# Two of three score banks to ScalarE, the third to VectorE, with new loads and planner constants, in a four-block attention kernel

## The chip, the cores and the metric

The kernel runs on one core of a Trainium2 chip. The metric is the device time of one execution in microseconds (us); lower is better. A core has engines that run side by side, each through its own list of instructions, in order: TensorE (PE, matrix products; PEld is its weight load), VectorE (DVE), ScalarE (ACT, functions such as exp), GpSimd (POOL), and the queues that start DMA transfers (SP, and ACT's own). An instruction waits on semaphores for what it needs, and everything behind it on its engine waits with it.

## The reference

x is 2048 x 1024 in bf16. Four blocks follow each other: A, B, A, B with the same weights for both A and for both B. Each has a layer normalisation before it and adds its result to x.

```
def A(x, wqkv, w_phi, wo):                  # linear attention, 32 heads of 32
    q, k, v = heads(x @ wqkv)
    pq, pk = q @ w_phi[h], k @ w_phi[h]
    phi_q = concat(softmax(pq), softmax(-pq));  phi_k likewise
    kv = phi_k^T v;  z = sum_s phi_k
    return ((phi_q kv) / (phi_q z + 1e-6)) @ wo
def B(x, wqkv, wo):                         # softmax attention, 32 heads of 32
    q, k, v = heads(x @ wqkv)
    return (softmax(q k^T / sqrt(32)) v) @ wo
```

## The kernel before

**One planner writes the order.** Nothing in the program is placed by hand. Each step is recorded as an `Op` with an engine, an assumed duration, dependencies, buffers and a priority. `Sched.run` then plays through time: an engine that is free takes the ready op of the lowest priority value whose buffers can be had, and the order in which it takes them is the order in which the instructions are emitted. On-chip memory is one arena from which buffers are cut, with a quota for each class; the accumulators are eight PSUM banks of 128 x 512 f32. The constants at the top (`LAT`, `act_us`, `dve_us`, `MM`, `MM4`) are what the planner assumes of latencies and durations. Where PE would be idle too long, the planner emits a filler: four column matmuls against a constant (`idle_acc` at L1377, or `idle` with onesD).

**Stages.** Work goes by chunks of 512 positions (four) and by groups of four heads (eight). In a linear block (A), `layernorm`, `a_keys`, `a_queries` and `a_out` run full 128 x 128 matmuls (helper line L481); q and k weights have w_phi folded in at the start (`fold_phi`: PE transposes L613, copies L617, products L636, evacuations L643 and L646). x comes in transposed by `load_x` (L516), chunk 0 first, chunks 1 to 3 in one piece for each of eight row blocks. The weights that PE transposes come on ACT's queue in two halves of rows (L604). Quota "mm" is the number of banks that the products of `a_queries` and `a_out` may hold.

**Attention (B).** Scores are computed transposed: keys on partitions, queries along the free dimension. A unit is one head, 128 keys, 512 queries: one matmul of 32 rows, one bank. A turn is a query chunk with a group of four heads, 64 units (two pairs of heads `pp`, eight key blocks `d`, four units `j`); there are 32 turns in each attention. Units are gathered by threes: three matmuls on three row strips (L1101) into banks 0 to 2 or 3 to 5 in turn, and one exponential of 1536 elements on ScalarE (L1110), into a buffer E. Products with v and the sums of the denominator are column matmuls, four at a time (L1142), accumulating in bank 6, which VectorE copies out at the end of each half turn (L1158). Bank 7 serves the projections that run beside attention (helper line L485).

**VectorE's share.** `EXTRA` names for each turn the pairs (pp, d) whose units j = 2 and 3 are not ScalarE's. `exp_dve` computes their exponentials on VectorE: for each of the two units a single score matmul into bank 7 (L1037), issued "along" a score group on another row strip, and a read that adds a bias and clamps (L1044); then for both together two integer steps (L1047, L1050), three polynomial steps (L1055) and a last product (L1058). The fields `along` and `rows` and the constants `AGAIN` and `DUE` make the planner place the single matmul beside a score group.

Of the kernel before, what the change touches and what calls it, by code (L numbers as in the profile page):

```python
# [10 lines left out]
ACT = mybir.ActivationFunctionType  # L11
# [23 lines left out]
class Op:  # L35
    __slots__ = ("eng", "dur", "lat", "fn", "bufs", "prio", "mode", "ndep", "out", "t", "start", "seq", "accum", "first", "ahead", "along", "drain", "rows")

    def __init__(self, eng, dur, lat, fn, bufs, prio, mode, seq):
        self.eng, self.dur, self.lat, self.fn, self.bufs = eng, dur, lat, fn, bufs
        self.prio, self.mode, self.seq = prio, mode, seq  # L40
        self.ndep, self.out, self.t, self.start, self.accum, self.first, self.ahead, self.along, self.drain = 0, [], 0.0, None, None, False, 0.0, False, False
        self.rows = ()


LAT = {"PE": 0.25, "ACT": 0.2, "DVE": 0.1, "POOL": 0.2, "SP": 2.0, "AQ": 2.0}
SWITCH = 0.1
AGAIN = 0.2
# [4 lines left out]
class Sched:  # L52
# [99 lines left out]
    def run(self):  # L152
# [21 lines left out]
        rows = ()  # L174
        started = {}
        for o in self.ops:
            if o.ndep == 0:
                heapq.heappush(ready[o.eng], (not (o.first or o.along), o.prio - o.ahead, o.seq, o))
        now = -100.0
        t, left, order = 0.0, len(self.ops), []  # L180
        while left:
            moved = False
            for e in engines:
# [5 lines left out]
                while ready[e] and len(skipped) < 400:  # L189
# [11 lines left out]
                    if item[3].along and (mode[e] != item[3].mode or item[3].rows[0] in rows) and item[3].prio > now - DUE:  # L201
                        skipped.append(item)
                        continue
# [25 lines left out]
                if pick.first:  # L229
                    now = pick.prio  # L230
# [5 lines left out]
                if pick.along and (mode[e] != pick.mode or pick.rows[0] in rows):  # L236
                    d += AGAIN
                if e == "PE":
                    rows = pick.rows
# [15 lines left out]
                heapq.heappush(events, (t + d, n, pick, True))  # L255
# [12 lines left out]
            while events and events[0][0] <= t + 1e-9:  # L268
                _, _, o, own = heapq.heappop(events)
                if not own:  # L270
                    for b in o.bufs:
                        b.left -= 1
                        if b.left == 0:
                            self._release(b)
                for x in o.out:
# [4 lines left out]
                    if x.ndep == 0:  # L280
                        heapq.heappush(ready[x.eng], (not (x.first or x.along), x.prio - x.ahead, x.seq, x))
# [15 lines left out]
DUE = 0.0  # L297
# [4 lines left out]
QUOTA = {"pk": 3, "pv": 2, "kv": 1, "ln": 2, "mm": 2, "cmp": 2, "bc": 4, "num": NUMS, "wt": 4, "fil": 2,  # L302
# [3 lines left out]
         "xs": 1, "xu": 2, "xg": 1, "xx": 1, "E1": 3}  # L306
# [14 lines left out]
EXTRA = (lambda i: [(0, 2), (1, 2)] if 10 <= i < 19 else [(1, 2)] if 2 < i < 31 else [],  # L321
         lambda i: [(0, 1), (0, 5), (1, 3)] if 10 <= i < 26 and i % 2 else [(0, 3), (1, 3)] if 1 <= i < 30 else [])


def act_us(n):
    return n / 1200 + 0.064


def dve_us(n):
    return n / 960 + 0.15  # L330


MM = 0.2165
# [3 lines left out]
def kernel(  # L337
# [150 lines left out]
    MM4 = 0.225  # L488
# [22 lines left out]
    def load_x():  # L511
        for lo, hi, prio, us in ((0, 1, -15.0, 1.3), (1, NC, -9.0, 2.0)):
            last = []
            for po in range(PO):
# [3 lines left out]
                    issue=us, kb=128))  # L518
# [8 lines left out]
    def layernorm(c, prio, banks, alone=False, n=2):  # L527
# [7 lines left out]
        for h in range(n):  # L535
# [6 lines left out]
            else:  # L542
                halves.append(op(
                    "DVE", 2048 / 1920 + 0.15, lambda hs=hs: nc.vector.tensor_tensor(
# [55 lines left out]
    def fold_phi(col, wd_v, prio, use_pe):  # L600
        w_t = []
        if use_pe:
            nb, nv = sb("wnat", PO, D)
            ld = [dma(-20.0, lambda h=h: nc.scalar.dma_start(  # L604
                out=nv()[:, 4 * h:4 * h + 4, :], in_=A_w[:, 4 * h:4 * h + 4, col:col + D]),
                (), [nb], q="AQ", kb=1024) for h in range(2)]
            for g in range(G):
                tb, tv = ps("wt", ANY)

                def tr(g=g, tv=tv):  # L610
# [4 lines left out]
                t1 = op("PE", 8 * 0.11, tr, ld, [tb, nb], prio, mode="n")  # L615
                wb, wv_ = sb("wT", D)
                t2 = op("ACT", act_us(1024), lambda tv=tv, wv_=wv_: nc.scalar.copy(  # L617
                    out=wv_(), in_=tv().bitcast(BF16)), [t1], [tb, wb], prio)
# [8 lines left out]
        for fc in range(2):  # L627
            s_b, s_v = sb("slab", PO, C512)
            parts = []
            for m in range(PO):  # L630
# [8 lines left out]
                a = op("PE", 4 * 0.1, fn, [w_t[4 * fc + k][2] for k in range(4)] + phi_ld,  # L639
# [384 lines left out]
    def exp_dve(qc, g, pp, d, prio, kT, q_of):  # L1024
# [7 lines left out]
        for k in range(2):  # L1032
            s_b, s_v = ps("xs", FIL)

            def sfn(k=k, s_v=s_v):
                r = slice(64 + 32 * k, 96 + 32 * k)
                nc.tensor.matmul(  # L1037
                    out=s_v(), lhsT=kT[g][1]()[r, pp, d * P:(d + 1) * P],
                    rhs=q_of[(qc, g)][1]()[r, (pp + 1) % 2, :], start=True, stop=True,
                    tile_position=(64 + 32 * k, 0))  # L1040
            so = op("PE", 0.05, sfn, flat([kT[g][2][d // 2], q_of[(qc, g)][2]]),
                    [s_b, kT[g][0], q_of[(qc, g)][0]], prio, mode="r")
            so.along, so.rows = True, (2 + k,)
            ys.append(op("DVE", dve_us(512), lambda k=k, s_v=s_v: nc.vector.tensor_scalar(  # L1044
                out=y_v()[:, k, :].bitcast(I32), in0=s_v(), scalar1=POW2_B, scalar2=0.0, op0=ALU.add, op1=ALU.max),
                [so], [s_b, y_b], prio + 0.01))
        mo = op("DVE", 1024 / 1920 + 0.15, lambda: nc.vector.tensor_scalar(  # L1047
            out=m_v().bitcast(I32), in0=y_v().bitcast(I32), scalar1=0x7FFFFF, scalar2=0x3F800000,
            op0=ALU.bitwise_and, op1=ALU.bitwise_or), ys, [y_b, m_b], prio + 0.02)
        po = op("DVE", 1024 / 1920 + 0.15, lambda: nc.vector.tensor_scalar(  # L1050
            out=y_v().bitcast(I32), in0=y_v().bitcast(I32), scalar1=0x7F800000, scalar2=None,
            op0=ALU.bitwise_and), [mo], [y_b], prio + 0.02)
        last = [mo]
        for i, c in enumerate(POW2_C):
            last = [op("DVE", dve_us(1024), lambda i=i, c=c: nc.vector.scalar_tensor_tensor(  # L1055
                out=x_v(), in0=(x_v() if i else m_v()), scalar=c, in1=m_v(), op0=ALU.add, op1=ALU.mult),
                last, [m_b, x_b], prio + 0.02)]
        eo = op("DVE", dve_us(1024), lambda: nc.vector.scalar_tensor_tensor(  # L1058
            out=e_v(), in0=x_v(), scalar=POW2_0, in1=y_v(), op0=ALU.add, op1=ALU.mult),
            [po, *last], [x_b, y_b, e_b], prio + 0.02)  # L1060
        return eo, (e_b, lambda: e_v().rearrange("p a b -> p (a b)"))

    def attention(base, kT, vT, q_of, gate, extra):
# [6 lines left out]
        ex_of, e_of = {}, {}  # L1070
        for qc, g in turns:
            for pp, d in extra(pos[(qc, g)]):
                eo, (e_b, e_v) = exp_dve(qc, g, pp, d, base + 10 * pos[(qc, g)] + 5 * pp + 0.5 * d - LEAD, kT, q_of)
                for k in range(2):
                    ex_of[(qc, g, pp, d, 2 + k)] = eo
                    e_of[(qc, g, pp, d, 2 + k)] = (e_b, e_v, k)
        units = [u for u in units if u not in ex_of]
        n = 0
        while units:
            grp = []  # L1080
            for u in units[:LOOK]:
                if len(grp) < WIDE and u[4] not in [v[4] for v in grp]:
                    grp.append(u)
            w = len(grp)
            units = [u for u in units if u not in grp]
# [327 lines left out]
```

## Time and profile before

| | us |
|---|---|
| median of three runs (2389.13 to 2389.97) | 2389.96 |
| profiled execution | 2389.32 |
| its span, first to last instruction | 2387.5 |
| PE busy | 2245.1 |
| ScalarE busy | 2077.7 |
| VectorE busy | 1646.7 |

Busy time is the union of an engine's instructions. Matmuls are pipelined and fillers count, so PE's figure is no measure of useful work; PE's busy time and matmul durations overlap from one to the next. Instructions of ScalarE overlap too: the duration of one is longer than the distance to the next. In a row of groups the columns are line, engine, operation, output and input, form, count, then busy us and mean ns of one, then the engine's idle time before them and what ended it. In a row of the timeline they are start, length, engine, line, operation, count, and idle time before.

### The profile page before, as it was taken

Reading aid. Unit: us, or ns where it says so; the run is one execution under the profiler, and the core shown is the slowest. Engines: PE = TensorE matmul, PEld = TensorE weight load, DVE = VectorE, ACT = ScalarE, POOL = GpSimd, SP = SyncE. Lnnn points to the kernel's source line nnn. Section 1 sums busy time; section 2 is a strip of 40 time slices with the busy share of each in tenths; the row PEclk is TensorE's granted clock in tenths of the full one; section 3 lists DMA queues with packets and bytes.
Section 4 is the critical chain, followed back from the end, with each engine's and each line's share of the span. In section 5 each row is a group of like instructions: output and inputs, shape, how many; then the busy total and the mean of one; then the engine's idle time right before and its main releaser. Section 6 shows DMA issues by size and latency. Waiting matters only on the chain.

```text
span 2387.5 us, 65441 instructions
## 1 busy us (share of the span) xinstructions
PE 2245.1 (94%) x28960; PEld 845.8 (35%) x28960; DVE 1646.7 (69%) x2107; ACT 2077.7 (87%) x1856; POOL 25.7 (1%) x70
## 2 busy tenths in 40 slices
PE   7999999999999999999998999999999999989998
PEld 4443343333333333333333434433333333333333
DVE  6987752345577767666665776477778888978763
ACT  6336549999999999999997555899999999999998
POOL 0000000000000000000000000000000000000000
PEclk9999999999999999999999999999999999999999
DMA  9120101112231121222413101011111100111111
GB/s 213 50 50 1 32 14 36 30 38 54 57 90 55 46 69 55 81 68 81 130 57 107 37 5 32 22 32 31 34 26 37 37 20 24 55 36 34 39 36 37
DMA packets 216805, 118.58 MB, mean 50 GB/s; under 512 B 138952, under 2 KB 206536, under 8 KB 215752
## 3 DMA queue, kind: packets, MB, share of 16 engines
q1 hardware_dynamic: 215464, 112.29, 17.6%
q8 instruction: 226, 3.70, 0.6%
q10 hardware_dynamic: 1056, 2.10, 0.3%
q14 instruction: 59, 0.48, 0.1%
HBM read 78.71 MB, written 14.14 MB: 39 GB/s over the span
## 4 chain that ended last, share of the span: by engine, by line
ACT 45%; PE 33%; issue 10%; DVE 7%; DMA 3%; SPq 2%; ACTq 0%; DVEq 0%
ACT arena L1110 42%; PE psum L481 17%; PE psum L485 5%; PE psum L1142 4%; PE psum L1101 4%; DMA arena<-rd 2%; DVE arena L1055 2%; ACT arena L685 1%; SPq L516 1%; DVE arena L1199 1%; DMA arena<-arena 1%; DVE arena L1044 1%; PE psum L854 1%; PE psum L718 1%; DVE arena L577 0%
## 5 line engine op out<-in xcount | busy, mean ns | idle before, releaser
L1110 ACT ACTIVATE arena<-psum 128x1536 bf16<-128x1536 f32 x1297 | 1751.5, 1687 | 21.1 <-PE psum L1101 17.0
L1142 PE MATMUL psum<-arena 128*32 128x512 bf16 x4096 | 627.4, 385 | 10.6 <-DVE arena L1158 9.3
L1142 PE MATMUL psum<-arena,ones_bf 128*32 128x512 bf16 x4096 | 627.6, 385 | 0.0
L1101 PE MATMUL psum<-arena 32*128 32x512 bf16 x3890 | 512.6, 383 | 84.6 <-ACT arena L1110 74.3
L485 PE MATMUL psum<-arena 128*32 128x512 bf16 (+1 forms) x8768 | 581.2, 376 | 9.3 <-DVE arena L917 3.6
L481 PE MATMUL psum<-arena 128*128 128x512 bf16 (+1 forms) x2032 | 454.9, 374 | 13.6 <-ACT arena L685 4.4
L1101 PEld LDWEIGHTS <-arena 32*128 32x128 bf16 x3890 | 173.8, 91 | 586.9 <-issue 576.1
L1055 DVE SCALAR_TENSOR_TENSOR arena<-arena 128x1024 f32<-128x1024 f32 x309 | 377.0, 1220 | 4.3
L481 PEld LDWEIGHTS <-arena 128*128 128x128 bf16 x2032 | 190.5, 98 | 255.3 <-issue 55.5
L485 PEld LDWEIGHTS <-arena 128*32 128x32 bf16 x8768 | 195.7, 96 | 237.5 <-issue 117.1
L1142 PEld LDWEIGHTS <-arena 128*32 128x32 bf16 x4096 | 167.0, 95 | 252.1 <-issue 196.5
L1044 DVE TENSOR_SCALAR arena<-psum 128x512 int32<-128x512 f32 x206 | 141.8, 688 | 94.0 <-PE psum L1037 81.5
L917 DVE CAST arena<-psum 128x512 bf16<-128x512 f32 x120 | 82.6, 689 | 168.8 <-PE psum L485 153.5
L1142 PEld LDWEIGHTS <-ones_bf 128*32 128x32 bf16 x4096 | 163.7, 95 | 30.9 <-issue 12.1
L1058 DVE SCALAR_TENSOR_TENSOR arena<-arena 128x1024 bf16<-128x1024 f32 x103 | 125.7, 1221 | 4.1 <-PE psum L1142 0.2
L1377 PE MATMUL psum<-xT,zero 128*32 128x512 bf16 x1412 | 114.4, 381 | 0.0
L685 ACT ACTIVATE arena<-psum 128x512 bf16<-128x512 f32 x80 | 42.9, 600 | 82.1 <-PE psum L481 65.6
L689 DVE TENSOR_REDUCE arena<-arena 128x32 f32<-128x1024 bf16 x64 | 77.8, 1215 | 44.5 <-ACT arena L685 44.1
L1199 DVE TENSOR_TENSOR arena<-arena 64x512 bf16<-64x512 f32 x124 | 84.7, 683 | 33.5 <-DMA arena<-rd 31.9
L1158 DVE COPY arena<-psum 128x512 f32<-128x512 f32 x126 | 86.3, 685 | 26.3 <-PE psum L1142 25.8
L811 ACT ACTIVATE arena<-psum 128x512 bf16<-128x512 f32 x128 | 69.5, 595 | 33.3 <-PE psum L481 32.7
L573 DVE TENSOR_TENSOR arena<-xT,arena 128x1024 f32<-128x1024 bf16 x64 | 77.9, 1220 | 24.2 <-ACT arena L562 24.0
(101 smaller groups left out, 1363.3 us busy)
## 6 DMA issues: line engine op xcount, KB each, us to landing
arena<-rd SPq DMA_DIRECT2D x62, 256.0 KB
arena<-in_B_wqkv_dram SPq DMA_DIRECT2D x48, 256.0 KB
arena<-in_A_wqkv_dram SPq DMA_DIRECT2D x10, 1024.0 KB
arena<-arena SPq DMA_DIRECT2D x256, 32.0 KB
arena<-in_B_wo_dram SPq DMA_DIRECT2D x32, 256.0 KB
arena<-wd_k SPq DMA_DIRECT2D x8, 1024.0 KB
arena<-arena SPq DMA_DIRECT2D x96, 64.0 KB
arena<-in_B_wqkv_dram SPq DMA_DIRECT2D x4, 1024.0 KB
```

What stands on the lines that cost most here:

```text
L481: nc.tensor.matmul(out_, lhsT=lhsT, rhs=rhs, start=start, stop=stop, skip_group_check=True)
L485: nc.tensor.matmul(out_[ks, :], lhsT=lhsT[:, ks], rhs=rhs, start=start, stop=stop, tile_position=(0, 32 * k), skip_group_check=True)
L917: return op("DVE", dve_us(512), lambda: nc.vector.tensor_copy(out=dst(), in_=src()), [dep], bufs, prio)
L1044: ys.append(op("DVE", dve_us(512), lambda k=k, s_v=s_v: nc.vector.tensor_scalar(out=y_v()[:, k, :].bitcast(I32), in0=s_v(), scalar1=POW2_B ...
L1055: last = [op("DVE", dve_us(1024), lambda i=i, c=c: nc.vector.scalar_tensor_tensor(out=x_v(), in0=(x_v() if i else m_v()), scalar=c, in1=m_ ...
L1058: eo = op("DVE", dve_us(1024), lambda: nc.vector.scalar_tensor_tensor(out=e_v(), in0=x_v(), scalar=POW2_0, in1=y_v(), op0=ALU.add, op1=ALU ...
L1101: nc.tensor.matmul(out=s_v()[:, x * C512:(x + 1) * C512], lhsT=kT[g][1]()[r, pp, d * P:(d + 1) * P], rhs=q_of[(qc, g)][1]()[r, (pp + j // ...
L1110: ex = op("ACT", act_us(w * C512), lambda s_v=s_v, e_v=e_v, w=w: nc.scalar.activation(out=e_v()[:, 0:w * C512], in_=s_v(), func=ACT.Exp, s ...
L1142: nc.tensor.matmul(out=a_v()[col:col + 32, :], lhsT=v_v()[:, kc % 4, o:o + DH] if what == 0 else ones_bf[:], rhs=ev()[:, x * C512:(x + 1) ...
L1158: cp = op("DVE", dve_us(512), lambda t_v=t_v, a_v=a_v: nc.vector.tensor_copy(out=t_v(), in_=a_v()), [last], [a_b, t_b], prio - 4)
L1199: s = [op("DVE", dve_us(512), lambda a=a, k=k, o_v=o_v, r_v=r_v, T=T: nc.vector.tensor_tensor(out=o_v()[a, :], in0=T[k][1]()[a, :], in1=r_ ...
L1377: nc.tensor.matmul(psum[32 * k:32 * k + 32, 6 * C512:7 * C512], lhsT=zero[:], rhs=xT[:, 0, 0:C512], start=False, stop=False, tile_position ...
```

## The change

- **Score groups.** A unit of VectorE's no longer has a bank and a matmul of its own. Any three units make a group, with at most one of VectorE's among them, and that one is put last, in the group's third bank. ScalarE's exponential then covers the first two banks (1024 elements) and VectorE's read takes the third, at the priority of the bank evacuations. `along`, `rows`, `AGAIN`, `DUE` and buffer class "xs" go.
- **VectorE's share.** `EXTRA` gives (0, 1) and (1, 1) to nearly every turn: 51 pairs in the first attention (37 before) and 60 in the second (66 before).
- **Durations.** The planner's constants are new, among them the fixed part of a VectorE instruction (0.067 us for 0.15) and of a ScalarE instruction (0.052 for 0.064), the latencies from ScalarE and VectorE to others (0.17 for 0.2, 0.18 for 0.1), and a latency of an engine to itself (`OWN`), which was none.
- **Loads.** x's chunk 0 gets a priority ahead of the phi loads, chunk 1 is loaded by itself, chunks 2 and 3 together. W's two halves are column halves, so that a transpose group waits for one half. VectorE takes every other evacuation of these transposes.
- **Banks.** The quota "mm" is 4 in place of 2.

```diff
-LAT = {"PE": 0.25, "ACT": 0.2, "DVE": 0.1, "POOL": 0.2, "SP": 2.0, "AQ": 2.0}
+LAT = {"PE": 0.25, "ACT": 0.17, "DVE": 0.18, "POOL": 0.2, "SP": 2.0, "AQ": 2.0}
+OWN = {"PE": 0.0, "ACT": 0.15, "DVE": 0.1, "POOL": 0.1, "SP": 0.0, "AQ": 0.0}
...
-                    if item[3].along and (mode[e] != item[3].mode or item[3].rows[0] in rows) and item[3].prio > now - DUE:
-                        skipped.append(item)
-                        continue
...
-                heapq.heappush(events, (t + d, n, pick, True))
+                heapq.heappush(events, (t + d, n, None, True))
+                n += 1
+                heapq.heappush(events, (t + d + OWN[e], n, pick, True))
...
-"mm": 2
+"mm": 4
...
-EXTRA = (lambda i: [(0, 2), (1, 2)] if 10 <= i < 19 else [(1, 2)] if 2 < i < 31 else [],
-         lambda i: [(0, 1), (0, 5), (1, 3)] if 10 <= i < 26 and i % 2 else [(0, 3), (1, 3)] if 1 <= i < 30 else [])
+EXTRA = (lambda i: [(0, 1), (1, 1)] if 8 <= i < 31 else [(1, 1)] if 2 < i < 31 else [],
+         lambda i: [(0, 1), (1, 1)] if 1 <= i < 31 else [])
 def act_us(n):
-    return n / 1200 + 0.064
+    return n / 1200 + 0.052
 def dve_us(n):
-    return n / 960 + 0.15
+    return n / 960 + 0.067
-MM = 0.2165
+MM = 0.2157
-    MM4 = 0.225
+    MM4 = 0.215
...
-        for lo, hi, prio, us in ((0, 1, -15.0, 1.3), (1, NC, -9.0, 2.0)):
+        for lo, hi, prio, us, kb in ((0, 1, -24.0, 1.3, 128), (1, 2, -9.0, 1.3, 400), (2, NC, -8.0, 2.0, 800)):
...
-                out=nv()[:, 4 * h:4 * h + 4, :], in_=A_w[:, 4 * h:4 * h + 4, col:col + D]),
+                out=nv()[:, :, C512 * h:C512 * h + C512], in_=A_w[:, :, col + C512 * h:col + C512 * h + C512]),
...
-                t1 = op("PE", 8 * 0.11, tr, ld, [tb, nb], prio, mode="n")
+                t1 = op("PE", 8 * 0.1, tr, [ld[g // 4]], [tb, nb], prio, mode="n")
...
+                if g % 2:
+                    t2 = op("DVE", dve_us(1024), lambda tv=tv, wv_=wv_: nc.vector.tensor_copy(
+                        out=wv_(), in_=tv().bitcast(BF16)), [t1], [tb, wb], prio)
...
+        def by_dve(u):
+            return u[:4] in ours and u[4] >= 2
...
-                if len(grp) < WIDE and u[4] not in [v[4] for v in grp]:
+                if len(grp) < WIDE and u[4] not in [v[4] for v in grp] and not (
+                        by_dve(u) and any(by_dve(v) for v in grp)):
                     grp.append(u)
+            units = [u for u in units if u not in grp]
+            grp.sort(key=by_dve)
             w = len(grp)
+            wa = sum(not by_dve(u) for u in grp)
...
-            so = op("PE", 0.24, sfn, deps + (gate if n == 0 else []), [s_b, *bufs], prio - 2, mode="r")
+            so = op("PE", 0.222, sfn, deps + (gate if n == 0 else []), [s_b, *bufs], prio - 2, mode="r")
...
-            ex = op("ACT", act_us(w * C512), lambda s_v=s_v, e_v=e_v, w=w: nc.scalar.activation(
-                out=e_v()[:, 0:w * C512], in_=s_v(), func=ACT.Exp, scale=math.log(2) / BITS),
+            ex = op("ACT", act_us(wa * C512), lambda s_v=s_v, e_v=e_v, w=wa: nc.scalar.activation(
+                out=e_v()[:, 0:w * C512], in_=s_v()[:, 0:w * C512], func=ACT.Exp, scale=math.log(2) / BITS),
...
+                if by_dve(u):
+                    read, rest, _, de_b, de_v = pair[u[:4]]
+                    read(u[4] - 2, so, s_b, lambda s_v=s_v, x=x: s_v()[:, x * C512:(x + 1) * C512], prio - 2)
```

In the changed file the score matmuls are L1094, the exponential L1102, the read of the third bank L1029, the two integer steps L1036 and L1039, the polynomial L1044 and L1047, the products with v L1143.

117 lines of the change are left out of this document (52 added, 65 removed).

## The prediction

> **What bounds the kernel now.** I read the page first, then busy time by stage, then the groups by line, then single stretches of the timeline.
>
> ```profile
> span 2387.5 us, 65441 instructions
> ACT  6336549999999999999997555899999999999998
> ACT 45%; PE 33%; issue 10%; DVE 7%; DMA 3%; SPq 2%; ACTq 0%; DVEq 0%
> ...
> 0.00:356.00 356.00, 334.33 (x2951) 151.14 (x2952) 264.49 (x364) 180.38 (x291) 11.04 (x38) 0.99 0.26 60
> 356.00:1287.40 931.40, 875.53 (x12748) 308.65 (x12747) 562.93 (x710) 916.19 (x718) 12.10 (x24) 0.99 0.24 66
> 1287.40:1506.00 218.60, 210.44 (x1581) 89.26 (x1580) 154.86 (x213) 117.53 (x201) 2.58 (x8) 1.00 0.08 25
> 1506.00:2376.00 870.00, 818.02 (x11628) 294.13 (x11626) 657.75 (x812) 862.33 (x646) 0.00 (x0) 1.00 0.13 33
> ...
> L1110 ACT ACTIVATE arena<-psum 128x1536 bf16<-128x1536 f32 x1297 | 1751.5, 1687 | 21.1 <-PE psum L1101 17.0 <-PE psum L1142 3.4 <-PE psum L1037 0.3
> L1377 PE MATMUL psum<-xT,zero 128*32 128x512 bf16 x1412 | 114.4, 381 | 0.0
> ```
>
> The stage rows give the stretch, then busy time of PE, weight load, VectorE, ScalarE, GpSimd. There are four stages: the linear layer (0 to 356), attention, the second linear layer (1287 to 1506), attention. In both attentions ScalarE is busy 916 of 931 us and 862 of 870; the chain names ScalarE's exponential (L1110) first, and its idle time in the whole run is 21.1 us. PE is busy nearly as long by the row, but 1412 of its matmuls (L1377) are filler against zeros. So attention lasts as long as ScalarE's work plus its stalls, and a linear stage as long as PE's work plus PE's waits.
>
> **Sum, term 1: ScalarE's exponentials.** Duration (1687 ns) is not pitch, because one starts before the last has ended. Runs of one form give the pitch.
>
> ```profile
> 1688.65 19.00 ACT L1110 ACTIVATE arena<-psum 128x1536 bf16<-128x1536 f32 x14
> 43.13 3.02 ACT L685 ACTIVATE arena<-psum 128x512 bf16<-128x512 f32 x6
> L685 ACT ACTIVATE arena<-psum 128x512 bf16<-128x512 f32 x80 | 42.9, 600 | 82.1 <-PE psum L481 65.6 <-issue 12.7 <-POOL arena L703 3.6
> ```
>
> Fourteen of 1536 in 19.00 us, less one duration, over 13: 1.332 us each. Six of 512: (3.02 - 0.60)/5 = 0.484. The slope between them puts 1024 elements at 0.908 (estimate). Units: 2 layers x 32 turns x 64 = 4096. Before, VectorE has 37 pairs of units in the first attention and 66 in the second (EXTRA), so ScalarE has 658 and 639 groups. After, VectorE has 51 and 60 pairs, and each of these units sits in a group that ScalarE covers by two thirds: in the written order of the changed program stand 580 of 1536 and 103 of 1024, then 562 and 121. First attention: -78 x 1.332 + 103 x 0.908 = -10.4 us. Second: -77 x 1.332 + 121 x 0.908 = +7.3. Net **-3.1**: nearly as many units, in 69 more instructions. The Trainium skill (ScalarE: Activation LUTs, "What ACT_TABLE_LOAD costs") gives 186 ns + 0.833 ns an element with 93 ns of overlap, that is 93 ns fixed where these rows leave 0.052; by it this term would be -0.9 and the sum 2 us more. The row of this case decides.
>
> **Term 2: the first loads.** The change sends chunk 0 of x ahead of the rest, chunk 1 by itself instead of with chunks 2 and 3, and W by column halves.
>
> ```profile
> 0.00:60.00 60.00, 42.84 (x383) 24.50 (x384) 36.24 (x72) 36.75 (x43) 2.64 (x12) 0.94 0.98 212
> 6.27 0.61 PE L613 MATMUL psum<-ident,arena 128*128 128x128 bf16 x4 [6.27 <-DMA arena<-in_A_wqkv_dram]
> 7.59 8.95 SPq L516 DMA_TRANSPOSE xT<-in_A_x_dram  x7
> 9.75 5.22 PE L613 MATMUL psum<-ident,arena 128*128 128x128 bf16 x52 [2.88 <-DMA arena<-in_A_wqkv_dram]
> 17.84 20.67 SPq L516 DMA_TRANSPOSE xT<-in_A_x_dram  x8
> 41.32 1.91 ACT L539 ACTIVATE arena<-xT 128x2048 bf16<-128x2048 bf16 x1 [3.21 <-DMA xT<-in_A_x_dram]
> 45.23 8.63 PE L481 MATMUL psum<-arena 128*128 128x512 bf16 x32 [4.38 <-ACT arena L685]
> ```
>
> Before, SP holds seven of chunk 0's transposes behind the four phi loads until 7.59. Chunk 1 lands only with all of x, ScalarE waits for it at 41.32 with key exponentials queued behind, and PE loses 4.38 us. After, SP's order is eight transposes, four phi loads, two V slabs, seven transposes of chunk 1, the store of the first folded slab, the eighth; by the issue row (8.95/7 = 1.28 us each) sixteen of them take 20.5 us, so chunk 1 is out some 10 us before 41.32 with the other loads between, and the 4.38 us go. What is late next is the store, which waits for folds, with chunk 1's last transpose queued behind it. Chunk 0 starts up to 5 us sooner, but W's halves now share the engines with it (DMA share 0.98 over these 60 us), which pushes the 6.27 up. The Trainium skill (DMA: Bandwidth & Descriptors, "Queues, rings and completion order") has each DMA engine go round robin between the queues; by it the 6.27 would up to double, the term would be near 0 and the sum 5 us more; no row of before has both queues busy long enough to tell. I take **-5**, bounds 0 (W's delay eats the 4.38) and -9 (both gains).
>
> **Term 3: the start of attention.** In the changed order 43 full matmuls that stood behind the first score group stand ahead of it, and 1.8 us of column groups: 43 x 0.217 + 1.8 = 11.1 us later, with 0.217 from the chain (104 in 22.57 us). Before, ScalarE ran beside that work, badly; the second row is L1110 alone:
>
> ```profile
> 332.86 22.57 PE psum L481 x104
> 355.40:392.80 37.40, 28.76 (x22) 1.00 0.13 29
> ```
>
> 22 exponentials are worth 22 x 1.332 = 29.3, so 8.1 of these 37.4 us were lost, and after nothing is mixed in there. **+3.0**, bounds -3 and +8. That ahead of it, the four banks ("mm" 4) let PE run past ScalarE's evacuations in the linear stages, where PE is idle 22 and 8 us of the stage rows, mostly for loads and chains that two more banks don't shorten: **-2**, bounds 0 and -7. The even split of the W copies over VectorE and ScalarE, and the new durations (0.600 for a 512 read, where before was 0.683), only reorder; I cost them nothing beside that, and VectorE's 264 of 356 us hide the copies.
>
> **Term 4: hand-off of the score banks.** New. Two score groups own three banks each; group n+2 may be written when group n has been read. ScalarE then needs it by the end of n+1.
>
> ```profile
> 798.54 15.07 ACT L1110 ACTIVATE arena<-psum 128x1536 bf16<-128x1536 f32 x11
> 800.22 0.39 PE L1101 MATMUL psum<-arena 32*128 32x512 bf16 x3 [0.19 <-ACT arena L1110]
> 800.55 0.39 PE L1142 MATMUL psum<-arena 128*32 128x512 bf16 x1
> 800.77 0.38 PE L1142 MATMUL psum<-arena 128*32 128x512 bf16 x1
> 801.57 0.40 PE L1101 MATMUL psum<-arena 32*128 32x512 bf16 x3 [0.19 <-ACT arena L1110]
> ```
>
> The exponential of 798.54 ends at 800.23; the score group starts there and is done at 800.62; the exponential after next begins at 798.54 + 2 x 1.338 = 801.22. Spare: 0.60 us, signal included. With a 1024 in between it is 0.60 - 0.42 = 0.18, and any PE work in the way becomes a stall. The short groups stand two by two (111 pairs), so PE must also turn a whole group round in 0.908. I counted PE's work from one score group to the next in the written order, at 0.22 for each four column matmuls (800.55 to 800.77) and for a score group, and 0.1 for each change between the two kinds (800.22 to 800.55 is 0.33): the 222 intervals after a short group hold 0.91 us on average, and 66 of them hold more than 0.908, by 18 us together. About half is taken up by the 0.18 and by the long group beside it: **+10**. Bounds 0, where nothing is in the way, and +55, two four-sets in the way each time: 222 x (0.43 - 0.18).
>
> **Term 5: VectorE's read sits in that hand-off.** Before, its scores have bank 7 and nobody of the exponential waits for them. After, the read of the third bank must end before PE writes the group after next, and PE's queue (PV, fillers, projections) stands behind that score group.
>
> ```profile
> L1055 DVE SCALAR_TENSOR_TENSOR arena<-arena 128x1024 f32<-128x1024 f32 x309 | 377.0, 1220 | 4.3
> L1044 DVE TENSOR_SCALAR arena<-psum 128x512 int32<-128x512 f32 x206 | 141.8, 688 | 94.0 <-PE psum L1037 81.5 <-ACT arena L1110 7.8 <-PE psum L1101 4.0
> L1047 DVE TENSOR_SCALAR arena<-arena 128x1024 int32<-128x1024 int32 x103 | 71.2, 691 | 7.3 <-PE psum L1142 1.8
> 900.00:1260.00 360.00, 333.61 (x5356) 122.44 (x5354) 241.89 (x298) 358.36 (x301) 12.10 (x24) 1.00 0.26 80
> ```
>
> A read (0.69) behind one running operation (up to 1.22) ends 1.9 us after its score; allowed are, from a score 0.5 us ahead of its exponential, 0.908 + 1.332 less score and signals (0.55), so 2.2, or 1.8 where the neighbour is short too. So a read is late only at a busy VectorE. A pair costs two reads, two integer steps and four polynomial steps, 2 x 0.69 + 2 x 0.69 + 4 x 1.22 = 7.6 us. The first attention gets 14 more pairs, 12 of them in its last twelve turns (one pair each before, two after; a turn is 931/32 = 29.1 us, so the 360 us below 1260 stand for them), where VectorE goes from 241.9 to 241.9 + 12 x 7.6 = 333 of 360 us. The second loses six. I take **+6**: 48 reads in those turns late by an eighth of a us. Bounds 0 and +25. The 206 single score matmuls that vanish (term of PE alone) cost ScalarE 0.3 us of idle by L1110's row: nothing to win.
>
> **Sum.** -3.1 - 5 + 3 - 2 + 10 + 6 = +9 on the profiled execution's 2389.3 us (span 2387.5 plus 1.8 around it; the median of runs is 2390.0): **2398 us**.
>
> **The rivals.** *Faster:* the new order knows the real durations, and hides every hand-off: 66 intervals are paid out of 0.6 us spares. Then terms 4 and 5 are 0, the loads give -9, the start 0, the banks -5, and old stalls shrink by 2: -3 - 9 - 5 - 2 = -19, **2370**. For it: ScalarE idles only 21 us now, so the hand-off works. Against it: 0.18 us of spare has no row of before. *VectorE becomes the bound* in the last twelve turns of the first attention. ScalarE has 60 units a turn instead of 62 there, 17.33 x 1.332 + 4 x 0.908 = 26.7 us instead of 20.67 x 1.332 = 27.5, so the stretch shrinks to 350 us; VectorE's is 333: 17 us spare over 48 reads. It decides once a read makes VectorE wait over 0.35 us for its score; L1044's row shows 94.0/206 = 0.46. At 0.9 a read (a short exponential) it costs 43 - 17 = +26 in place of the +6: +29 or **2418**. Against it: the waits of before came with an idle VectorE. *Nothing to tell:* terms 4 and 5 at a third, +5, cancel against -7 of the others: **2388**. That the change doesn't take place is excluded: the order holds the 222 short exponentials.
>
> **How the numbers follow.** Forecast 0.44, faster rival 0.30, VectorE rival 0.13, cancelling 0.13. About 0.2% (4.8 us) can be told from no change. The forecast's own range is 2390 to 2412; 0.03 of its chance lies below 2394.8, and 0.02 of the cancelling case below 2385.2. Faster: 0.30 + 0.02 = 0.32. Within: 0.13 + 0.03 - 0.02 = 0.14. Slower: 0.44 + 0.13 - 0.03 = 0.54. Range 2370 to 2422: the ends are the two rivals' times, the upper with 4 us for a term 4 above its +10; the rest of that term's bound needs PE work in the way every time, and is left outside with what is left of the chances.
>
> **What would show it.** Right: L1102's idle time above 35 us, ended by score matmuls (L1094), whose own waits name VectorE's read (L1029) for some us; long pitch 1.33 and short 0.91; no 4 us gap of PE near 45; first exponential at 356 to 362; second attention longer by 10 to 20, first within 10. Wrong: idle of L1102 at 20 or less (faster rival), or VectorE busy over 58 of 60 us late in the first attention with ScalarE waiting (VectorE rival).

## The result, and the profile after

| | median, us | runs | lowest, highest | ratio to before, 95% |
|---|---|---|---|---|
| before | 2389.96 | 7 | 2388.57, 2391.78 | |
| after | 2396.74 | 7 | 2392.38, 2398.47 | 1.0023 [1.0013, 1.0033] |

The change makes the kernel 0.23% slower, +7 us where +9 was forecast. First the page of the kernel after (span, ScalarE's slices), then its busy time by stage, in the columns of the stage rows of before: stretch, PE, weight load, VectorE, ScalarE, GpSimd, granted clock, DMA share, GB/s.

```profile
span 2393.9 us, 68486 instructions
ACT  5436549999999999999997555899999999999998
...
0.00:357.30 357.30, 339.51 (x2981) 154.92 (x3022) 265.65 (x373) 177.74 (x291) 12.82 (x38) 1.00 0.26 61
357.30:1289.20 931.90, 889.78 (x13232) 309.13 (x13231) 648.25 (x817) 908.17 (x737) 16.60 (x24) 0.99 0.24 67
1289.20:1503.60 214.40, 209.31 (x1554) 89.44 (x1578) 152.05 (x213) 116.44 (x203) 2.30 (x8) 0.99 0.07 21
1503.60:2382.50 878.90, 851.08 (x12447) 300.25 (x12446) 613.48 (x764) 872.02 (x690) 0.00 (x0) 1.00 0.12 33
...
900.00:1260.00 360.00, 337.36 (x5430) 123.07 (x5426) 314.31 (x388) 347.46 (x305) 16.60 (x24) 0.99 0.27 81
```

The reader is to see three things. Both attentions are still ScalarE's (908 of 932 us, 872 of 879). The second linear stage is 4 us shorter, and the second attention 9 us longer. In the last twelve turns of the first attention VectorE is at 314 of 360 us, not at its end. Cut at the first and last exponential of each attention, the spans differ like this (us):

| | to first exponential | first attention | second linear stage | second attention | rest |
|---|---|---|---|---|---|
| before | 355.9 | 931.5 | 218.7 | 869.8 | 11.5 |
| after | 357.3 | 931.9 | 214.3 | 878.9 | 11.5 |
| difference | +1.4 | +0.4 | -4.4 | +9.1 | 0.0 |

Next are the groups of the kernel after: ScalarE's exponential (L1102) and VectorE's read of a third bank (L1029) by line, then the two shapes of the exponential apart.

```profile
L1102 ACT ACTIVATE arena<-psum 128x1536 bf16<-128x1536 f32 (+1 forms) x1366 | 1753.5, 1469 | 27.9 <-PE psum L1094 19.0 <-PE psum L1143 3.9 <-DVE arena L1200 2.5
L1029 DVE TENSOR_SCALAR arena<-psum 128x512 int32<-128x512 f32 x222 | 151.8, 686 | 102.3 <-PE psum L1094 96.8 <-ACT arena L1102 1.5 <-ACT arena L680 1.3
```

```profile
L1102 ACT ACTIVATE arena<-psum 128x1536 bf16<-128x1536 f32 x1142 | 1562.4, 1535 | 24.8 <-PE psum L1094 16.5 <-PE psum L1143 3.9 <-DVE arena L1200 2.5
L1102 ACT ACTIVATE arena<-psum 128x1024 bf16<-128x1024 f32 x224 | 234.3, 1131 | 3.1 <-PE psum L1094 2.6
```

The exponential's idle time rises only from 21.1 to 27.9 us. It hides the rest: an exponential that starts late often starts before the last one has ended on the record, so nothing counts as idle. Pitch shows it. The undisturbed pitch is 1.331 us (1536 elements) and 0.904 (1024). What each pitch from an exponential to ScalarE's next instruction has beyond that, added up, I call stalls: 22.0 and 12.8 us before (first, second attention), 36.3 and 14.8 after. The first attention is then -10.7 us of exponentials (-78 x 1.331 + 103 x 0.904), +14.3 of stalls and -3.2 of the rest; the second +7.3 of exponentials (-76 x 1.331 + 120 x 0.904, since one of the 639 groups of before was short already), +2.0 of stalls, -0.2 of the rest. PE's waits of the kernel after (total us, times, longest):

```profile
PE psum L1094 <- ACT arena L1102: 39.2, 164, 0.9
...
PE psum L1143 <- DVE arena L1159: 7.8, 8, 2.4
PE psum L1094 <- DVE arena L1029: 4.6, 8, 1.0
```

A score group (L1094) waits for VectorE's read of its bank eight times in the run. The start of the timeline, PE alone, and a stretch of all engines with short groups:

```profile
7.01 3.60 PE L604 MATMUL psum<-ident,arena 128*128 128x128 bf16 x32 [7.01 <-DMA arena<-in_A_wqkv_dram]
13.54 3.59 PE L604 MATMUL psum<-ident,arena 128*128 128x128 bf16 x32 [2.94 <-DMA arena<-in_A_wqkv_dram]
32.43 15.28 PE L472 MATMUL psum<-arena 128*128 128x512 bf16 x69 [0.42 <-DVE arena L568]
```

```profile
1698.91 7.48 ACT L1102 ACTIVATE arena<-psum 128x1536 bf16<-128x1536 f32 x6
1703.79 0.69 DVE L1029 TENSOR_SCALAR arena<-psum 128x512 int32<-128x512 f32 x1 [4.47 <-PE psum L1094]
1704.79 0.39 PE L1094 MATMUL psum<-arena 32*128 32x512 bf16 x3
1705.68 0.39 PE L1094 MATMUL psum<-arena 32*128 32x512 bf16 x3
```

W's second half lands later than before (13.54, not 9.75), and the 4.38 us gap of PE near 45 is gone: the row of 69 matmuls runs from 32.43 to 47.71 without a gap. In the second block two score groups start 0.89 us apart, as fast as a short exponential allows.

### The profile page after: what moved, and what is told of

It reads as the page before. It is cut to its first block, busy times and chain, and to the rows that moved or that the text cites. A ratio compares the mean times of both kernels' runs of the same rounds, so it can differ in the third digit from the quotient of the medians.

```text
span 2393.9 us, 68486 instructions
## 1 busy us (share of the span) xinstructions
PE 2296.1 (96%) x30267; PEld 856.3 (36%) x30336; DVE 1686.0 (70%) x2175; ACT 2075.6 (87%) x1921; POOL 31.7 (1%) x70
## 4 chain that ended last, share of the span: by engine, by line
ACT 33%; PE 23%; issue 8%; DVE 7%; DMA 4%; SPq 0%; ACTq 0%; DVEq 0%
ACT arena L1102 32%; PE psum L472 7%; PE psum L476 6%; PE psum L1143 4%; PE psum L1094 4%; DMA arena<-rd 3%; DVE arena L1044 2%; DVE arena L1029 1%; ACT arena L680 1%; DMA arena<-arena 1%; PE psum L1378 1%; DVE arena L1159 1%; DVE arena L1200 1%; DVE arena L1036 0%; DVE arena L1039 0%
## 5 line engine op out<-in xcount | busy, mean ns | idle before, releaser
L1102 ACT ACTIVATE arena<-psum 128x1536 bf16<-128x1536 f32 (+1 forms) x1366 | 1753.5, 1469 | 27.9 <-PE psum L1094 19.0
L1143 PE MATMUL psum<-arena 128*32 128x512 bf16 x4096 | 627.4, 384 | 9.0 <-DVE arena L1159 7.8
L1143 PE MATMUL psum<-arena,ones_bf 128*32 128x512 bf16 x4096 | 627.6, 384 | 0.0
L476 PE MATMUL psum<-arena 128*32 128x512 bf16 (+1 forms) x8768 | 584.5, 375 | 8.6 <-DVE arena L912 3.3
L1094 PE MATMUL psum<-arena 32*128 32x512 bf16 x4096 | 541.0, 384 | 50.0 <-ACT arena L1102 39.2
L472 PE MATMUL psum<-arena 128*128 128x512 bf16 (+1 forms) x1971 | 443.9, 373 | 11.4 <-issue 3.3
L1044 DVE SCALAR_TENSOR_TENSOR arena<-arena 128x1024 f32<-128x1024 f32 x333 | 405.0, 1216 | 4.3
L1094 PEld LDWEIGHTS <-arena 32*128 32x128 bf16 x4096 | 163.2, 91 | 596.7 <-issue 588.2
L476 PEld LDWEIGHTS <-arena 128*32 128x32 bf16 x8768 | 196.6, 96 | 237.4 <-issue 119.4
L1143 PEld LDWEIGHTS <-arena 128*32 128x32 bf16 x4096 | 162.2, 95 | 244.1 <-issue 195.4
L1029 DVE TENSOR_SCALAR arena<-psum 128x512 int32<-128x512 f32 x222 | 151.8, 686 | 102.3 <-PE psum L1094 96.8
L1143 PEld LDWEIGHTS <-ones_bf 128*32 128x32 bf16 x4096 | 158.9, 95 | 30.0 <-issue 13.9
L476 PE MATMUL psum<-xT,onesD 128*32 128x512 bf16 x1700 | 162.3, 381 | 1.7 <-DVE arena L936 1.6
L1047 DVE SCALAR_TENSOR_TENSOR arena<-arena 128x1024 bf16<-128x1024 f32 x111 | 135.0, 1216 | 5.0 <-PE psum L1094 1.7
L1378 PE MATMUL psum<-xT,zero 128*32 128x512 bf16 x1596 | 137.7, 382 | 0.2 <-DVE xT L987 0.2
L806 ACT ACTIVATE arena<-psum 128x512 bf16<-128x512 f32 x128 | 70.2, 604 | 27.9 <-PE psum L472 27.7
```

Of the source, the lines that this page charges most:

```text
L472: nc.tensor.matmul(out_, lhsT=lhsT, rhs=rhs, start=start, stop=stop, skip_group_check=True)
L476: nc.tensor.matmul(out_[ks, :], lhsT=lhsT[:, ks], rhs=rhs, start=start, stop=stop, tile_position=(0, 32 * k), skip_group_check=True)
L1029: o = op("DVE", dve_us(512), lambda: nc.vector.tensor_scalar(out=y_v()[:, k, :].bitcast(I32), in0=src(), scalar1=POW2_B, scalar2=0.0, op0= ...
L1047: return op("DVE", dve_us(1024), lambda: nc.vector.scalar_tensor_tensor(out=e_v(), in0=x_v(), scalar=POW2_0, in1=y_v(), op0=ALU.add, op1=A ...
L1094: nc.tensor.matmul(out=s_v()[:, x * C512:(x + 1) * C512], lhsT=kT[g][1]()[r, pp, d * P:(d + 1) * P], rhs=q_of[(qc, g)][1]()[r, (pp + j // ...
L1102: ex = op("ACT", act_us(wa * C512), lambda s_v=s_v, e_v=e_v, w=wa: nc.scalar.activation(out=e_v()[:, 0:w * C512], in_=s_v()[:, 0:w * C512] ...
```

## The experiments

Three theories stood at the start: the hand-off of short groups costs what the prediction had (terms 4 and 5); it costs little, and the planner's new constants lost the time by the order that they produce; or the parts don't add up, because every edit makes the planner write the whole order anew. The kernels are of two sorts. In some the order is planned again; in the others the instructions stay in the order of the kernel after, and a named one is left out or added as it is emitted. This table has them all; "stalls" are as above, for the two attentions.

| kernel | median, us | ratio to before, 95% | first exp. | 1st att. | 2nd lin. | 2nd att. | stalls |
|---|---|---|---|---|---|---|---|
| p_loads | 2389.73 | 1.0000 [0.9990, 1.0009] | 348.3 | 938.5 | 218.9 | 870.9 | 27.9, 13.8 |
| p_banks | 2383.03 | 0.9973 [0.9964, 0.9982] | 360.1 | 926.7 | 214.3 | 869.7 | 18.9, 12.6 |
| p_durs | 2412.61 | 1.0104 [1.0081, 1.0126] | 348.0 | 946.2 | 220.2 | 880.2 | 37.4, 23.2 |
| p_all3 | 2391.92 | 1.0005 [0.9996, 1.0014] | 357.7 | 929.9 | 213.9 | 877.2 | 25.5, 20.2 |
| q_nodur | 2385.60 | 0.9983 [0.9973, 0.9992] | 353.1 | 929.2 | 212.5 | 872.7 | 33.0, 8.3 |
| h_poly1 | 2388.04 | 0.9985 [0.9975, 0.9994] | 357.8 | 926.3 | 215.0 | 877.2 | 30.7, 13.1 |
| h_long | 2481.37 | 1.0385 [1.0368, 1.0403] | 356.5 | 964.6 | 214.6 | 931.2 | 17.0, 9.8 |
| h_nofill | 2442.41 | 1.0218 [1.0198, 1.0238] | 357.5 | 944.0 | 215.5 | 918.1 | 48.4, 54.1 |
| q_lat | 2409.43 | 1.0081 [1.0066, 1.0096] | 359.6 | 938.8 | 213.8 | 882.6 | 42.2, 20.9 |
| q_dur | 2399.33 | 1.0033 [1.0020, 1.0046] | 348.0 | 935.4 | 217.8 | 883.6 | 34.4, 19.5 |
| best1 | 2394.39 | 1.0022 [1.0012, 1.0031] | 357.8 | 931.5 | 213.7 | 872.5 | 31.6, 8.1 |
| best2 | 2428.77 | 1.0168 [1.0150, 1.0186] | 358.5 | 926.6 | 213.4 | 908.2 | 26.7, 56.6 |

The columns of stages and the stalls come from one profiled execution of each kernel. In most of these PE stands still once or twice in the first attention without a wait that the profile shows: the longest time is 2.8 us in after, 5.1 in p_loads, 3.8 in p_banks and 4.2 in best1, and in before there is none over 0.9. So a difference of a few us in the first attention of two rows says little by itself; the medians are of 4 to 25 runs.

**The parts one by one.** Before with the loads alone (`load_x` in three pieces, W by column halves, W copies split over two engines):

```
-for lo, hi, prio, us in ((0, 1, -15.0, 1.3), (1, NC, -9.0, 2.0)):
+for lo, hi, prio, us, kb in ((0, 1, -24.0, 1.3, 128), (1, 2, -9.0, 1.3, 400), (2, NC, -8.0, 2.0, 800)):
...
```

> The kernel before with the new loads alone (x's chunk 0 first, chunk 1 by itself, W in column halves, every other W copy on VectorE). If the loads are what shortened the first linear stage: 6 to 9 us faster than before, 2381 to 2384, first exponential 6 to 9 us sooner, PE's 4.4 us gap near 45 us gone, the rest unchanged. Rival (the new durations or the four banks did it): within 3 us of before.

Nothing is gained: the first exponential comes 7.6 us sooner, and the first attention takes 7.0 longer. It isn't work that moved: PE has the same 2951 matmuls ahead of the first exponential as before. ScalarE's stalls there are 5.9 us longer, and one place holds most of that, where PE stands still from 1234.9 to 1240.0 and the profile names no wait:

```profile
PE psum L1146 <- issue: 5.1, 1, 5.1
```

Whether every execution loses the gain in this way one profile can't show; the medians, of ten and 25 runs, differ by 0.1 us.

Before with four banks alone:

```
-"mm": 2
+"mm": 4
```

> The kernel before with quota mm 4 in place of 2 alone. If the four banks are what shortened the second linear stage (218.7 to 214.3): about 4 us off each linear stage, 2382. Rival (nothing gained by banks): within 2 us of 2390.

This kernel has the lowest median of the study, 0.27% below before and clear of after; its interval overlaps that of q_nodur. The first linear stage is not shorter, as it was expected to be: the first exponential comes 4.2 us later and the first attention is 4.8 shorter, with 16 of the 39 full 128 x 128 matmuls that PE did in this attention now ahead of it. The second linear stage shrinks by 4.4 us, and by 3.2 to 6.2 us in every kernel with the four banks but q_dur (0.9). Its stage row shows PE busy for 212.0 of 214.3 us, where the row of before has 210.4 of 218.6:

```profile
1286.80:1501.10 214.30, 212.01 (x1581) 89.50 (x1580) 154.62 (x213) 117.78 (x202) 2.60 (x8) 0.99 0.11 35
```

The waits that go are short and of several kinds. In the second linear stage of before they add up to 8.6 us, with four banks to 2.8; of the 5.9 us of rows that disappear, 4.2 name VectorE and 1.7 ScalarE. The largest two of before:

```profile
PE psum L793 <- DVE arena L778: 1.8, 2, 1.3
...
PE psum L481 <- ACT arena L811: 1.2, 2, 0.7
```

Before with the planner's constants alone:

```
-LAT = {... "ACT": 0.2, "DVE": 0.1 ...}
+LAT = {... "ACT": 0.17, "DVE": 0.18 ...};  OWN = {... "ACT": 0.15, "DVE": 0.1 ...}
-act_us: n / 1200 + 0.064;  dve_us: n / 960 + 0.15
+act_us: n / 1200 + 0.052;  dve_us: n / 960 + 0.067
...
```

> The kernel before with the new planner constants alone (durations, latencies, the latency of an engine to itself). If the constants only reorder, as the prediction had it: within 5 us of 2390, with ScalarE's stalls in attention no larger than before (21 and 13 us beyond pitch). Rival (the constants and not the third bank brought the stalls of attention): 10 to 20 us slower.

The largest single effect: +22.7 us by the medians (by the ratio 19 to 30), with the work of before and nothing added but fillers. The first exponential comes 7.9 us sooner; the loss is in the attentions, +14.7 and +10.4. The profile is of the fastest of the four runs, 2407.83. Waits of PE and of ScalarE in this kernel, then PE's row of before that answers to the first of them:

```profile
PE psum L1147 <- DVE arena L1163: 29.5, 41, 3.1
...
PE psum L490 <- DVE arena L1049: 8.0, 17, 1.3
...
ACT arena L1115 <- PE psum L1106: 22.9, 23, 3.6
ACT arena L1115 <- PE psum L1147: 11.9, 15, 1.7
```

```profile
PE psum L1142 <- DVE arena L1158: 9.3, 27, 0.6
```

PE's products with v (L1147) wait 29.5 us for VectorE to copy out bank 6, where before they waited 9.3. PE's queue stands meanwhile, score groups with it, and ScalarE runs out of scores: its waits for L1106 are 22.9 us, for L1101 before 17.0. By pitch, 16.6 of the 60.6 us of stalls lie at such a wait for bank 6 or begin within 1.5 us behind it, where before it was 1.0 of 34.8. In the trace of after, one VectorE step of 512 elements follows another after 0.60 us; the old constants have 0.683 for it and the new ones 0.600. That the old ones left a margin behind such steps would explain the late copies; this is argued, not shown.

All three parts together, still without the third bank:

```
 p_loads + p_banks + p_durs
```

> The kernel before with loads, banks and constants together: the change without the third bank. If the third bank costs what terms 1, 4 and 5 say (less 3 and plus 16): the changed kernel's 2397 less 13 to 18, so 2379 to 2384. Rival (third bank costs nothing, constants do): 2393 to 2399. Rival (third bank gains): above 2399.

0.0 - 6.5 + 22.7 would be +16; measured is +1.2. So the parts don't add up. From this kernel to after, the third bank and its EXTRA are all that is added, and they cost 4.3 us by the ratios (uncertain by some 3), not the 13 to 18 that terms 1, 4 and 5 would have.

**The constants within the change.** After with all constants of before:

```
-LAT, OWN, act_us, dve_us, MM, MM4 of after
+LAT, act_us, dve_us, MM, MM4 of before, OWN all 0
```

> The changed kernel with the planner's constants of before (loads, four banks and third bank stay). If the constants bring most of the new stalls, as 23 us for them alone on the kernel before suggest: 10 to 20 us off the changed kernel, 2377 to 2387. Rival (the third bank's hand-off brings them, as the prediction had it): 2394 to 2400.

Faster than before by 0.17%, with the third bank in place: the intervals of this kernel and of after don't meet, and the constants cost some 10 us. In the two profiled executions 8.9 us of that are in the attentions and 4.2 ahead of the first exponential, where after has 22 more of the full matmuls, 1.8 in the second linear stage, and the end gives 4.0 back. There is less idle time ahead of the short exponentials (0.6 us, not 3.1) and of the long ones (20.3, not 24.8):

```profile
L1102 ACT ACTIVATE arena<-psum 128x1536 bf16<-128x1536 f32 x1142 | 1570.0, 1633 | 20.3 <-PE psum L1094 14.6 <-PE psum L1143 2.4 <-DVE arena L1044 2.1
L1102 ACT ACTIVATE arena<-psum 128x1024 bf16<-128x1024 f32 x224 | 241.2, 1217 | 0.6 <-PE psum L1094 0.3
```

Half of the constants each: q_lat has the old latencies and the new durations, q_dur the reverse.

```
 q_lat:  -LAT, OWN of after                  +LAT of before, OWN all 0
 q_dur:  -act_us, dve_us, MM, MM4 of after   +those of before
```

> The changed kernel with only the latencies of before (LAT, and no OWN); its new durations stay. If the new durations, which leave the planner no margin, bring the stalls: still 2392 to 2399. Rival (the latencies do): 2384 to 2389, like the kernel with all constants of before.

> The changed kernel with only the durations of before; its new latencies and OWN stay. If the durations without margin bring the stalls: 2384 to 2389. Rival (the latencies do): 2392 to 2399.

Each half undone leaves the kernel no faster than after (2409 and 2399, against 2397 with both new and 2386 with both old). So which constant does it stays open, and whether it is the lost margin too: q_dur has the long VectorE durations again and gains nothing. Only the set as a whole can be priced. One part of the way is seen in the traces: stalls at late copies of bank 6, counted as above, are 9.1 us in after, 6.5 in p_all3 and 6.1 in q_lat and in q_dur, and 1.0 in before, 0.6 in p_banks and 2.0 in q_nodur. It is a part only (9.1 of 51.1 us in after), and best2 below has 11.2 with the old constants.

**The hand-off, with the order held.** VectorE's last polynomial steps are recorded, timed by the planner and placed, but two of three are not issued, so that VectorE is done sooner everywhere:

```
-last = [op(..., lambda i=i, c=c: nc.vector.scalar_tensor_tensor(...
+last = [op(..., lambda i=i, c=c: None if i else nc.vector.scalar_tensor_tensor(...
```

> The changed kernel, its order held, with two of the three polynomial steps of VectorE's exponential not issued (so these exponentials are wrong): 222 instructions of 1.22 us less on VectorE, nothing else moved. If PE waits for a late VectorE (third-bank read, copy of bank 6, evacuation of bank 7): 10 to 18 us faster than the changed kernel, 2379 to 2387, mostly in the first attention. Rival (PE's own work in the way of short groups): within 4 us of 2397.

-8.7 us against after by the medians, between the two expectations; in the profiled executions it is 6.2, of which 5.6 in the first attention and 1.7 in the second. Yet PE's score groups wait for the read as before:

```profile
PE psum L1143 <- DVE arena L1159: 6.8, 9, 2.4
PE psum L1094 <- DVE arena L1029: 3.8, 7, 0.9
```

So a late VectorE is worth 6 to 9 us, about the 6 of term 5, but only 0.8 of it goes by the wait that the term named, and 1.0 by the wait for bank 6. No single row holds the rest; where it goes stays open.

Each short exponential followed by one more of 512 elements, so that ScalarE's turn is long again:

```
 nc.scalar.activation(out=e_v()[:, 0:w * C512], ...)
+if more: nc.scalar.activation(out=e_v()[:, w * C512:(w + 1) * C512], in_=s_v()[:, 0:C512], ...)
```

> The changed kernel, its order held, with a second exponential of 512 after each short one (bank 0 once more, result not used), so that no group is short: 222 x 0.48 = 106 us more work for ScalarE. If shortness itself costs the hand-off (23 us by the trace around short groups): 75 to 85 us slower than the changed kernel. Rival (shortness costs nothing): 100 to 106 us slower.

```profile
L1103 ACT ACTIVATE arena<-psum 128x1536 bf16<-128x1536 f32 x1142 | 1581.0, 1652 | 9.9 <-PE psum L1094 4.3 <-PE psum L1147 2.7 <-DVE arena L1204 2.2
L1103 ACT ACTIVATE arena<-psum 128x1024 bf16<-128x1024 f32 x224 | 277.6, 1240 | 2.2 <-PE psum L1094 2.2
```

There are 222 additions (two of the 224 short exponentials have no third bank), of a median pitch of 0.478 us, worth 106 us; the time rises by 84.6. So some 21 us of after's stalls go when no group is short, and the idle time ahead of long exponentials falls from 24.8 to 9.9 us. Not all of it need come from the shortness: a ScalarE with more to do also hides stalls of other causes, and the 26.8 us left here are fewer than the 34.8 of before, which has no group of two banks but one. Counted in the trace of after, the 329 pitches with a short group one or two places ahead have 29.7 us of stalls, where as many pitches among long groups have 6.1 (at each attention's own rate): 23.6 us, by another road.

No fillers at all, order held:

```
 def idle_acc():
+    return
```

(likewise `idle`.)

> The changed kernel, its order held, with no filler matmul issued (800 sets of four). If fillers stand in the way of score groups: 5 to 12 us faster than the changed kernel. Rival (fillers stand where PE waits anyway): within 3 us, unless the granted clock falls, then slower.

Not a way out: +46 us against after. The rows of most of the two attentions and the clock in 40 slices:

```profile
356.00:1300.00 944.00, 861.70 (x11976) 287.53 (x11971) 649.03 (x817) 910.12 (x736) 16.57 (x24) 0.94 0.24 66
1520.00:2430.00 910.00, 825.79 (x10424) 265.47 (x10428) 610.36 (x758) 873.33 (x685) 0.00 (x0) 0.88 0.12 31
...
PEclk9999999999987989999998999999887887889989
```

The granted clock falls from 0.99 and 1.00 to 0.94 and 0.88, and a matmul takes longer with it, as the same group of after and of h_nofill shows (384 and 417 ns each):

```profile
L1143 PE MATMUL psum<-arena,ones_bf 128*32 128x512 bf16 x4096 | 627.6, 384 | 0.0
```

```profile
L1143 PE MATMUL psum<-arena,ones_bf 128*32 128x512 bf16 x4096 | 690.3, 417 | 0.0
```

What fillers cost by standing in the way of score groups is less than what their absence costs.

**Towards a faster kernel.** Before with four banks and the third bank (with its EXTRA), old loads and old constants:

```
 q_nodur, with
-load_x in three pieces, W by column halves
+load_x in two pieces, W by row halves
```

> The kernel before with four banks and the third bank (with its EXTRA), loads and constants as before: against the kernel with four banks alone (2383) it tells the third bank's own price. If the hand-off is cheap once the planner has its margins: 2379 to 2384 (exponentials -3 us, some stalls). Rival (the third bank costs 10 us or more by itself): 2390 to 2398.

2394.4, so 11.7 us of ratio behind p_banks (0.9973 to 1.0022): this is the price of the third bank alone, with the planner's margins as they were. That it would be cheap then is refuted. The stages give first attention +4.8, second +2.8, the end +4.6, and the linear stages -2.9. The end is work that moved: behind the last exponential stand three rounds of column matmuls for the last projections (L476), where p_banks has one.

The same with 15 more pairs for VectorE in the second attention, where VectorE has room:

```
-lambda i: [(0, 1), (1, 1)] if 1 <= i < 31 else []
+lambda i: [(0, 1), (1, 1)] + [(0, 5)] * (i % 2) if 1 <= i < 31 else []
```

> The run with four banks and third bank, with 15 more pairs for VectorE in the second attention (three in every odd turn). Thirty short groups more, 30 x 0.42 = 13 us less for ScalarE there. If VectorE has the room (613 + 114 of 870 us): 7 to 13 us faster than without, near 2373. Rival (late reads and copies give it back): within 3 us of that run.

```profile
L1098 ACT ACTIVATE arena<-psum 128x1536 bf16<-128x1536 f32 x1112 | 1531.0, 1570 | 58.8 <-PE psum L1139 43.9 <-PE psum L1090 11.5 <-DVE arena L1043 2.2
L1098 ACT ACTIVATE arena<-psum 128x1024 bf16<-128x1024 f32 x254 | 266.8, 1164 | 2.5 <-PE psum L1090 2.4
```

34 us slower than best1. ScalarE waits 43.9 us for products with v (L1139) to give an E buffer back, not for scores. Why they stand so late in this order was not followed up.

## Why the prediction came out

The total held, in part by luck: terms were off in opposite ways, and the price of a part depends on what stands in the kernel already. The steps of the change, each on top of the last, from the ratios (0.001 is 2.4 us, and each step is uncertain by some 3 us):

| step | from, to | us | prediction |
|---|---|---|---|
| four banks | before, p_banks | -6.5 | -2 |
| third bank, new EXTRA | p_banks, best1 | +11.7 | +13 (terms 1, 4, 5) |
| loads | best1, q_nodur | -9.3 | -2 (term 2, -5, and the start of attention, +3) |
| constants | q_nodur, after | +9.6 | 0 |
| sum | before, after | +5.5 | +9 |

In another order the prices are others: the loads cost nothing as the first step, and the third bank 4.3 us as the last. Its 11.7 here agrees with terms 1, 4 and 5 partly by chance, since 4.6 of it lies behind the last exponential, where no term had put anything.

**Term 1** held: pitch 1.331 and 0.904 where 1.332 and an estimate of 0.908 were taken, and -10.7 and +7.3 us where -10.4 and +7.3 stood. The fixed part of an exponential that reads PSUM is 0.05 us here. The Trainium skill (ScalarE: Activation LUTs, "What ACT_TABLE_LOAD costs") comes to 93 ns, for a tile whose memory it does not name; the term that follows from it, some -0.8 us, would have been too small.

**Term 2** named the right things: the 4.38 us gap of PE went, and W's halves came later, at 7.01 and 13.54. The Trainium skill (DMA: Bandwidth & Descriptors, "Queues, rings and completion order") has the engines alternate between the queues; the trace agrees in direction, but the first half came 12% later, far from double, and no run separates the queues from the new shape of the halves. The price has no fixed value: 0 by itself, -9.3 here.

**Term 3**'s start of attention came out at 357.3 us, within its 356 to 362, and its mechanism is in the trace: 39 full matmuls stood in the first attention before and none does after, and the stalls of its first 22 exponentials fall from 4.6 us to 0.1. The 8.1 us that the term took as lost hold ScalarE's other work too. No experiment prices it by itself: four banks alone move 16 of the 39 ahead, and the constants the last 22. Of the four banks the size failed: -2 was taken because PE's idle time in the linear stages seemed to be loads and chains, while 4.4 us of the second stage went with two more banks, mostly waits for VectorE. It lay inside the bound of -7.

**The constants** are the step that failed: "only reorder; I cost them nothing". They cost about 10 us within the change and 22.7 alone, and the prediction gave them neither a bound nor a rival on the slow side. Reordering is not free when the order is static: nothing at run time corrects a queue in which the wrong step stands first.

**Term 4** (+10) was too small for the kernel as it is: 21 to 24 us around short groups, within the bound of 55, with whatever of term 5 falls there. With the old constants the same count gives 9 (q_nodur) and 7 (best1), where terms 4 and 5 together had 16. **Term 5** (+6) held in size (h_poly1, 6 to 9) and not in its way: eight waits of 4.6 us in all name the read.

**The rivals.** *Faster* needed the new durations to hide the hand-offs; they did the reverse. But q_nodur, the change without them, is faster than before, so the sign hung on the edit that was costed at nothing. *VectorE the bound* is refuted: 314 of 360 us, and PE's score groups wait 4.6 us for its reads in the whole run. The 333 worked out added up durations, but VectorE's steps overlap as ScalarE's do: 0.69 us is the duration of a step of 512 elements, 0.60 its pitch. *Cancelling* came nearest of the three, with other terms than it named.

**What would show it.** The idle time of L1102 was put above 35 us and is 27.9, between the two marks: idle time doesn't hold a late start that overlaps the last one's end, and the pitch sums do. The second attention grew by 9.1, just short of the 10 to 20. The first grew by 0.4, within its 10.

## What to carry to other kernels

Where a planner writes a static order, an edit of its assumed durations is a change of the whole order, and durations nearer the truth can give a slower one: here one such edit moved the time by 10 and by 23 us, so bound it by tens of us on a kernel like this, on both sides, and try it by itself. Read stalls by pitch where instructions overlap, since idle time shows only a part. Parts of a change to such a kernel don't add up: the four banks alone (2383 us) beat both kernels, and the sum of three single trials missed their price together by 15 us.

## What the runs showed of the hardware

The granted clock fell without any long pause of PE. In h_nofill the longest stretch without a matmul in the second attention is 1.2 us, by the modelled ends of all its records, and PE is busy for 825.8 of 910 us; yet the granted clock there is 0.88, and 1.00 with fillers. These are means: the clock record of the trace holds full and half speed alone, the half in pieces of one to seven times 3.41 us. In the 3.41 us ahead of each of the 34 falls within the run PE had a matmul running for at most 0.67 of the time (median 0.58); of the 579 other such pieces at full speed, nine had as little, and their median is 1.00. The Trainium skill (TensorE: Matmul & The Clock Gate, "Part 1: The HAM clock gate") names in its table of states an idle window of about 3.4 us for the lower clock; here windows with short pauses sufficed, and no pause of that length was needed. VectorE reading a bank next to those that ScalarE reads was no slower for it: 0.686 us, against 0.688 before from a bank apart.
